# Second layer: the down product in Strassen's seven products too, all up products of 1024 tokens ahead of it

## The chip, the core and the metric

The kernel runs on one core of a Trainium2 chip. The core has a matrix engine (TensorE, PE in the rows, PEld for its weight loads), three element-wise engines (VectorE = DVE, ScalarE = ACT, GpSimd = POOL), a queue engine (SyncE = SP) and 16 DMA engines. The metric is the device time in microseconds, the median of several runs. A profile is one further execution, taken by the hardware profiler; its instructions carry the lines of the kernel, as L642.

## The reference, cut to what matters

```
attn  = memory attention of q, k, v, phi            # 8 x 8 heads, 576 positions, 64 wide
x     = attn as (4608 tokens, 512)
x1    = (silu(x @ w_gate) * (x @ w_val)) @ w_out    # layer 1: 512 -> 1536 -> 512
h     = x1 @ w_in                                   # layer 2, "up":   512 -> 2048
g     = where(h > 0, h, exp(min(h, 0)) - 1)         # ELU
out   = g @ w_out2                                  # layer 2, "down": 2048 -> 512
```

Inputs come as 64-bit floats. The kernel makes 32-bit values of them on the chip and splits each operand of a product into a high and a low part, so that one product is three matmuls: high by high, high by low, low by high.

## The kernel before, in words

Matmuls take a stationary operand of 128 x 128 and a moving one of up to 512 columns, and add into one of eight accumulation banks of PSUM.

**Layer 1** runs over batches of 576 tokens in halves of 288 columns. A first pass over eight batches holds attention, too. Two more passes (the loop that ends in L603) take four blocks of 128 hidden columns each: `gate1`, `val1`, and, two units later (`LAG`), `down2`, which adds into four banks; L525 copies these, and L526 adds the copy to `p1_d` in memory by an accumulating DMA on GpSimd's queue. Between the units the list `conv` is worked off: weights of layer 1, then those of layer 2. For layer 2 `quad_b1`, `quad_b2` and `quad_t` make the seven combinations of a block of `w_in` (VectorE and ScalarE), and `down_w` splits a block of `w_out2` (ScalarE and, at L122 and L123, GpSimd). `store_w2` stores them to memory from ScalarE's queue.

**Layer 2** runs over groups of tokens: 512 tokens first (two halves of 256), then four times 1024 (two halves of 512). The up product is done by Strassen's scheme in Winograd's form: the tokens in two halves, the inputs in two halves of 256 and the hidden columns in pairs of 128 give 2 x 2 blocks, and seven block products take the place of eight. `load3` forms the seven combinations of activations, `fetch_up` brings the weights' (SP queue), and `quad` (L689 to L722) does one of eight steps of 256 hidden columns. A `product` is 6 matmuls, a step 42. Several products add up in the same bank: a partial sum that is needed alone is first copied out by ScalarE (L695, L702, L706), and VectorE adds the copy to another bank (L698, L711, L715). `elu` takes the minimum with zero on VectorE, Exp and Tanh on ScalarE, and a product and a maximum on VectorE.

The down product is plain: for each chunk of 128 tokens (stationary) 16 blocks of weights (moving, 512 output columns) add up in one bank, 3 matmuls a block. Its chunks for the first half of a group are issued between the products of `quad`; the second half's hidden values wait in SBUF (`g2`) and are done after the last step (L757 to L760). Outputs go from L680 or L682 by SP's queue. PSUM is shared as four banks for up products (`ps_up`) and four for down (`ps_acc3`).

The order on each engine is set when the program is built: instructions that are ready go in the order of the program, with those under `high_priority` first; each engine then executes its list strictly in order.

Of the kernel before, what the change touches and what calls it, by code (L numbers as in the profile page):

```python
# [8 lines left out]
F32 = mybir.dt.float32  # L9
# [20 lines left out]
PARTS = (0, 4), (4, 7)  # L30
NWA = 28
NWB = 8
# [5 lines left out]
def attention_moe_moe(ctx: ExitStack, tc: tile.TileContext, qT, phiT, kv, kv4, w1g, w1o, w2, out):  # L38
# [9 lines left out]
    wr_p = ctx.enter_context(tc.tile_pool(name="wr", bufs=4))  # L48
    wt_p = ctx.enter_context(tc.tile_pool(name="wt", bufs=2))
    wa_p = ctx.enter_context(tc.tile_pool(name="wa", bufs=NWA))  # L50
    vx_p = ctx.enter_context(tc.tile_pool(name="vx", bufs=4))
    vt_p = ctx.enter_context(tc.tile_pool(name="vt", bufs=B))
# [21 lines left out]
    up_d = [[dram.tile([128, 2 * (z - a) * 256], F32, name=f"upd{q}_{a}") for a, z in PARTS] for q in range(NQD)]  # L74
    dn_d = [dram.tile([128, 2, DM], F32, name=f"dnd{u}") for u in range(NU2)]
# [17 lines left out]
    def load_w(store, u, i, src, pool, split=True, own=False, raw=None, parts=None):  # L93
# [3 lines left out]
        if parts:  # L97
            pass
        elif split:
            hi = pool.tile([128, 512], F32R, tag="w", name="whi")  # L100
            lo = pool.tile([128, 512], F32R, tag="w", name="wlo")
        else:
            full = pool.tile([128, 512], F32, tag="w", name="wg")
# [3 lines left out]
        with tc.issue_after(last["h"].ins) if "h" in last else nullcontext():  # L107
# [7 lines left out]
            if parts:  # L115
                for part, cs in parts:
                    tt(out=part, in0=v[:, cs], in1=cf[:, cs], op=ALU.add)
                return
            if split:
                act(out=hi, in_=v, func=AF.Copy)  # L120
                part = tt if own else nc.gpsimd.tensor_tensor
                part(out=v, in0=v, in1=hi.bitcast(F32), op=ALU.subtract)  # L122
                part(out=lo, in0=v, in1=cf, op=ALU.add)  # L123
            else:
                tt(out=full, in0=v, in1=cf, op=ALU.add)
        store[u][i] = (hi, lo) if split else full
# [3 lines left out]
    WO = [[None] for _ in range(NU1)]  # L130

    def load_wg(p, k, pool):
        load_w(WG, p, k, w1g[p, k], pool, False, raw=raw.pop((p, k), None))

    def load_wo(u, pool):
        load_w(WO, u, 0, w1o[u], pool, own=u < UA)

    QU = {}
# [7 lines left out]
    def quad_b1(q, pool):  # L146
        t = QU[q] = uq_p.tile([128, 7, 256], F32, tag="uq", name="uq")
        load_w(None, 0, 0, w2[2 * q, :, :1024], None, parts=[(t[:, :2].rearrange("p r c -> p (r c)"), slice(0, 512))])

    def quad_b2(q, pool):  # L150
        t = QU[q]
        b12 = QU[q, 1] = uq_p.tile([128, 256], F32, tag="b12", name="b12")
        load_w(None, 0, 0, w2[2 * q + 1, :, :1024], None, parts=[(b12, slice(0, 256)), (t[:, 4], slice(256, 512))])

    def quad_t(q, pool):
        t, b12 = QU.pop(q), QU.pop((q, 1))
        with tc.issue_after(last["h"].ins):
            tt(out=t[:, 2], in0=b12, in1=t[:, 0], op=ALU.subtract)
            tt(out=t[:, 3], in0=t[:, 4], in1=t[:, 2], op=ALU.subtract)
            tt(out=t[:, 5], in0=t[:, 4], in1=b12, op=ALU.subtract)  # L160
            tt(out=t[:, 6], in0=t[:, 1], in1=t[:, 3], op=ALU.subtract)
            for i, (a, z) in enumerate(PARTS):
                w = pool.tile([128, 2, z - a, 256], F32R, tag=f"u{i}", name="uw")
                act(out=w[:, 0], in_=t[:, a:z], func=AF.Copy)
                tt(out=w[:, 1], in0=t[:, a:z], in1=w[:, 0].bitcast(F32), op=ALU.subtract)
                stores.append((up_d[q][i], w.rearrange("p i r c -> p (i r c)").bitcast(F32)))

    def down_w(u, pool):
        w = [[None]]
        load_w(w, 0, 0, w2[u, :, 1024:], pool)  # L170
        for i in range(2):
            stores.append((dn_d[u][:, i], w[0][0][i].bitcast(F32)))
# [255 lines left out]
    def down1(b, hf, hs, m):  # L428
        ps = ps_gv.tile([128, HS], F32, tag="g", name="pd")
        for u in range(UA):  # L430
            down(ps, WO[u][0], hs[u], slice(128 * m, 128 * m + 128), u == 0, u == UA - 1)
# [13 lines left out]
    for b in range(B):  # L445
# [10 lines left out]
        if b == B - 2:  # L456
            wb_p = ctx.enter_context(tc.tile_pool(name="wb", bufs=NWB))
# [53 lines left out]
    up_p = ctx.enter_context(tc.tile_pool(name="up", bufs=2))  # L511
    st_uq = ExitStack()
    uq_p = st_uq.enter_context(tc.tile_pool(name="uq", bufs=1))

    def down2(q):
# [4 lines left out]
        for m in range(KD):  # L520
            down(accs[m], WO[u][0], hs, slice(128 * m, 128 * m + 128), first, last_u)
# [15 lines left out]
    def load3(t0, n, ops, kks):  # L537
        for kk in kks:
            A = []
            for i in range(2):  # L540
                r = wr_p.tile([128, 2, n], F32, tag="wr", name="x1l")
                for b, o, c0, c in tokens(t0 + i * n, n):
                    nc.sync.dma_start(out=r[:, :, c0:c0 + c], in_=p1_d[b][:, kk::2, o:o + c])
                A += [r[:, 0], r[:, 1]]
            a11, a12, a21, a22 = A
            s1, s2, s3, s4 = (wt_p.tile([128, n], F32, tag=t, name="xs") for t in ("wv", "wc", "wv", "wc"))
            tt(out=s1, in0=a21, in1=a22, op=ALU.add)
            tt(out=s2, in0=s1, in1=a11, op=ALU.subtract)

            def split(r, x):  # L550
                pool = xo_p if r == 6 and n == 512 else wa_p
                hi = pool.tile([128, n], F32R, tag="w", name="xhi")
                act(out=hi, in_=x, func=AF.Copy)
                lo = pool.tile([128, n], F32R, tag="w", name="xlo")
                tt(out=lo, in0=x, in1=hi.bitcast(F32), op=ALU.subtract)
                ops[r][kk] = hi, lo

            split(0, a11)
            split(1, a12)
            split(2, s1)  # L560
            split(3, s2)
            tt(out=s4, in0=a12, in1=s2, op=ALU.subtract)
            tt(out=s3, in0=a11, in1=a21, op=ALU.subtract)
            split(4, s4)
            split(5, s3)
            split(6, a22)

    def new_ops():
        return [[None] * 2 for _ in range(7)]

# [9 lines left out]
    xops = new_ops()  # L580
    for ps in range(2):
        for b in range(B):
            nb, np_ = (b + 1, ps) if b + 1 < B else (0, ps + 1)
            for hf in range(2):
# [3 lines left out]
                for u in range(UA * (ps + 1), UA * (ps + 2)):  # L588
# [8 lines left out]
                    if np_ == 2 and hf == 0 and u % 2 == 1:  # L597
                        load3(0, 256, xops, (u // 2 % 2,))
                    slot += 1
                    while conv and NCONV - len(conv) < slot * NCONV // 126:  # L600
                        conv.pop(0)()
                        if len(stores) > 2:
# [6 lines left out]
    st_p2.close()  # L609
# [187 lines left out]
```

## Time and profile before

| | us |
|---|---|
| median of 3 runs | 1536.23 |
| lowest, highest | 1535.06, 1536.71 |
| profiled execution, its time | 1537.9 |
| profiled execution, first to last instruction (span) | 1536.1 |

Mean granted clock of TensorE over the span: 0.984 of 2.4 GHz; by stretches of 40 us it was 0.74 and 0.83 in the first two, 0.91 from 640 to 680 us, 0.96 from 720 to 800, and 1.00 in all others up to 1520. Its two levels are 1.2 and 2.4 GHz.

How to read it: a row of a group of instructions names the line, the engine, the operation, what it writes and reads (out<-in), the shapes and the count; behind it stand the busy time of the group in us, the mean duration of one in ns, the idle time of the engine just before them, and what ended that. Matmuls overlap, so that their durations add up to more than the time that they take; the time of one is the distance of their starts. 1 KB is 1024 bytes.

### The profile page before, as it was taken

How to read it: one execution, taken by the hardware profiler on the slowest of the kernel's cores; microseconds unless marked ns; L12 is line 12 of the kernel's file. 1: busy time of each engine (PE TensorE's matmuls, PEld its weight loads, DVE VectorE, ACT ScalarE, POOL GpSimd, SP SyncE). 2: the span in 40 equal slices, each digit the busy share in tenths (PEclk: the TensorE clock that was granted, in tenths of full speed). 3: DMA queues.
4: the chain of work that ended last, by engine and by line, in shares of the span. 5: the costliest groups of instructions: out<-in, count | busy, mean ns of one | idle time of the engine just before them, and what ended most of it. 6: DMA issues, size and time to landing. Idle time of an engine off the chain costs nothing.

```text
span 1536.1 us, 25746 instructions
## 1 busy us (share of the span) xinstructions
PE 1478.1 (96%) x9768; PEld 1279.5 (83%) x9768; DVE 1041.3 (68%) x2000; ACT 760.6 (50%) x1579; POOL 109.2 (7%) x87
## 2 busy tenths in 40 slices
PE   4799999999999999989999999999999999999998
PEld 2578888899999999989888888888887888888887
DVE  7988678756666666655776876854677367826662
ACT  4555445544555555444555655633455345624451
POOL 0000000021220000134320000000000000000000
PEclk7899999999999999999999999999999999999999
DMA  9788322436568777878588866576567655566445
GB/s 374 257 293 282 129 94 101 164 126 160 137 162 216 193 188 229 248 209 228 131 251 316 305 213 217 202 266 209 180 209 247 226 180 208 192 231 222 165 135 180
DMA packets 124059, 317.83 MB, mean 207 GB/s; under 512 B 12832, under 2 KB 44576, under 8 KB 114720
## 3 DMA queue, kind: packets, MB, share of 16 engines
q1 hardware_dynamic: 90912, 264.80, 49.9%
q0 software_dynamic: 16896, 18.88, 8.7%
q10 hardware_dynamic: 16128, 32.51, 5.6%
q8 instruction: 77, 1.26, 0.3%
q14 instruction: 46, 0.38, 0.1%
HBM read 245.89 MB, written 70.25 MB: 206 GB/s over the span
## 4 chain that ended last, share of the span: by engine, by line
PE 79%; DVE 6%; DMA 3%; ACT 1%; issue 1%; POOL 0%; ACTq 0%; DVEq 0%; SPq 0%; POOLq 0%
PE acc L675 8%; PE acc L674 8%; PE acc L676 8%; PE pu L642 7%; PE pu L644 7%; PE pu L643 7%; PE acc L203 4%; PE acc L204 4%; PE acc L205 4%; PE pg L198 3%; PE pv L198 3%; PE pg L200 2%; PE pv L200 2%; PE pv L199 2%; PE pg L199 2%; PE pvw L186 2%
## 5 line engine op out<-in xcount | busy, mean ns | idle before, releaser
L675 PE MATMUL acc<-dnw,hh 128*128 128x512 f32 x576 | 224.4, 390 | 0.0
L674 PE MATMUL acc<-dnw,hh 128*128 128x512 f32 x576 | 218.5, 390 | 0.3 <-ACT o L682 0.3
L676 PE MATMUL acc<-dnw,hl 128*128 128x512 f32 x576 | 212.4, 389 | 0.0
L642 PE MATMUL pu<-xhi,upw 128*128 128x512 f32 (+1 forms) x560 | 206.2, 370 | 5.6 <-DVE cc L711 2.6
L643 PE MATMUL pu<-xlo,upw 128*128 128x512 f32 (+1 forms) x560 | 206.4, 369 | 0.0
L644 PE MATMUL pu<-xhi,upw 128*128 128x512 f32 (+1 forms) x560 | 205.5, 369 | 0.0
L209 ACT ACTIVATE hh<-g 128x512 fp32r<-128x512 f32 (+1 forms) x160 | 92.5, 587 | 162.5 <-PE acc L675 106.8
L211 DVE TENSOR_TENSOR hl<-g,hh 128x512 fp32r<-128x512 f32 (+1 forms) x160 | 100.9, 635 | 104.6 <-ACT hh L209 94.6
L203 PE MATMUL acc<-hh,whi 128*128 128x288 f32 x512 | 153.0, 300 | 4.0 <-ACT p1a L525 4.0
L651 ACT ACTIVATE e<-g 128x512 f32<-128x512 f32 (+1 forms) x160 | 90.8, 584 | 132.4 <-DVE g L650 131.3
L230 DVE SCALAR_TENSOR_TENSOR h<-s,pv 128x288 f32<-128x288 f32 x192 | 86.4, 450 | 102.5 <-PE pv L200 77.6
L204 PE MATMUL acc<-hh,wlo 128*128 128x288 f32 x512 | 151.3, 296 | 0.0
L205 PE MATMUL acc<-hl,whi 128*128 128x288 f32 x512 | 150.6, 296 | 0.0
L653 DVE SCALAR_TENSOR_TENSOR g<-e,g 128x512 f32<-128x512 f32 (+1 forms) x160 | 100.6, 640 | 59.1 <-ACT g L652 58.5
L209 ACT ACTIVATE hh<-h 128x288 fp32r<-128x288 f32 x192 | 84.9, 442 | 112.0 <-DVE h L230 108.7
L211 DVE TENSOR_TENSOR hl<-h,hh 128x288 fp32r<-128x288 f32 x192 | 94.2, 491 | 53.8 <-ACT hh L209 53.5
L198 PE MATMUL pg<-at,vw 128*128 128x288 f32 x384 | 119.2, 310 | 11.0 <-ACT at L354 5.7
L642 PEld LDWEIGHTS pu<-xhi,upw 128*128 128x128 f32 x560 | 106.1, 190 | 26.0 <-DVE cc L711 2.8
L674 PEld LDWEIGHTS acc<-dnw,hh 128*128 128x128 f32 x576 | 108.0, 188 | 22.6 <-ACT o L682 0.7
L675 PEld LDWEIGHTS acc<-dnw,hh 128*128 128x128 f32 x576 | 108.2, 188 | 22.2 <-DMA dnw<-dnd 0.4
L676 PEld LDWEIGHTS acc<-dnw,hl 128*128 128x128 f32 x576 | 108.0, 188 | 21.9
L643 PEld LDWEIGHTS pu<-xlo,upw 128*128 128x128 f32 x560 | 106.2, 190 | 18.2
(112 smaller groups left out, 3347.5 us busy)
## 6 DMA issues: line engine op xcount, KB each, us to landing
dnw<-dnd SPq DMA_DIRECT2D x288, 256.0 KB, 3.6
upw<-upd SPq DMA_DIRECT2D x40, 1024.0 KB, 6.9
upw<-upd SPq DMA_DIRECT2D x40, 768.0 KB, 5.1
at<-atd SPq DMA_DIRECT2D x16, 1152.0 KB, 7.2
p1d<-p1a POOLq DMA_DIRECT2D x32, 576.0 KB, 7.1
kvr<-kv SPq DMA_DIRECT2D x32, 512.0 KB, 6.5
wr<-w SPq DMA_DIRECT2D x32, 512.0 KB, 4.8
wr<-w1g SPq DMA_DIRECT2D x24, 512.0 KB, 4.7
```

The lines of the kernel that those rows point to most:

```text
L198: mm(ps, lhsT=wh, rhs=ah, start=g == 0, stop=False)
L203: mm(ps, lhsT=w[0][:, ms], rhs=hs[0], start=start, stop=False)
L204: mm(ps, lhsT=w[1][:, ms], rhs=hs[0], start=False, stop=False)
L205: mm(ps, lhsT=w[0][:, ms], rhs=hs[1], start=False, stop=stop)
L209: act(out=hh, in_=h, func=AF.Copy)
L211: tt(out=hl, in0=h, in1=hh.bitcast(F32), op=ALU.subtract)
L642: mm(ps, lhsT=wh, rhs=xh, start=start and kk == 0, stop=False, skip_group_check=not start)
L643: mm(ps, lhsT=wh, rhs=xl, start=False, stop=False, skip_group_check=not start)
L644: mm(ps, lhsT=wl, rhs=xh, start=False, stop=kk == 1, skip_group_check=not start)
L674: mm(acc, lhsT=hh, rhs=wh, start=u == 0, stop=False)
L675: mm(acc, lhsT=hh, rhs=wl, start=False, stop=False)
L676: mm(acc, lhsT=hl, rhs=wh, start=False, stop=u == NU2 - 1)
```

## The change

- **Tokens.** The first group becomes 512 tokens by the plain scheme, up and down, with activations as moving operand of 512 columns. The four groups of 1024 tokens stay.
- **Order.** In each group all eight up steps come first; the ELU's outputs of all four blocks stay in SBUF (`G`, four tiles). Then seven steps down, one for each of Strassen's products over hidden columns in two halves of 1024: per product 8 blocks of 128 hidden columns x 2 halves of the outputs x 3 matmuls. Here weights are stationary, activations move, and the output is transposed; the host transposes it back. What were chunks of the down product between the up products is gone from there.
- **Within an up step** the products go P1, P5, P6, P2, P3, and P7 and P4 follow between those of the next step. P1, P6, P7 and P4 add up in one bank.
- **Element-wise passes are twice as wide** (1024 columns). The minimum becomes a Relu with scale -1 on ScalarE. The split of hidden values (`split2`) moves into the down steps, and so do the combinations of hidden values (`AFTER`).
- **Weights.** Blocks of `w_out2` get seven combinations like those of `w_in`: `set_load` and `set_split` for both, on VectorE and ScalarE; GpSimd's subtraction and sum are left for blocks of layer 1 alone. 60 tasks instead of 52 are spread over 118 units instead of 126. Fetches are of 1 MB or 768 KB into four buffers.
- **Memory.** SBUF's pools of layer 1 are closed ahead of layer 2 and new ones opened over them; PSUM is shared as six and two banks. A new pool waits until all of the pools that it overlaps are done with. Outputs go by GpSimd's queue.

The diff, cut to its core:

```diff
-        [lambda f=f, q=q: f(q, up_p) for q in range(NQD) for f in (quad_b1, quad_b2, quad_t)] + \
-        [lambda u=u: down_w(u, wb_p) for u in range(NU2)]
+        [lambda f=f, a=a: f(*a) for kind in ("up", "down") for q in range(NQD)
+         for f, a in ((set_load, (kind, q, 0)), (set_load, (kind, q, 1)), (set_split, (kind, q)))]
...
+    def set_split(kind, q):
+        t = SET.pop((kind, q))
+        with tc.issue_after(last["h"].ins):
+            tt(out=t[:, 0:7:6], in0=t[:, 4:6], in1=t[:, 2:5:2], op=ALU.subtract)
+            tt(out=t[:, 1], in0=t[:, 5], in1=t[:, 0], op=ALU.subtract)
+            tt(out=t[:, 7], in0=t[:, 3], in1=t[:, 1], op=ALU.subtract)
+            for r in (0, 4):
+                w = up_p.tile([128, 4, 2, 256], F32R, tag="u", name="uw")
+                act(out=w[:, :, 0], in_=t[:, r:r + 4], func=AF.Copy)
+                tt(out=w[:, :, 1], in0=t[:, r:r + 4], in1=w[:, :, 0].bitcast(F32), op=ALU.subtract)
...
+    def elu(c, src=None):
...
+            act(out=a, in_=c, func=AF.Relu, scale=-1.0)
...
+        act(out=e, in_=a, func=AF.Exp, scale=-1.0)
+        act(out=a, in_=a, func=AF.Tanh, scale=-0.5)
+        stt(out=a, in0=e, scalar=1.0, in1=a, op0=ALU.add, op1=ALU.mult)
...
+            tt(out=c, in0=a, in1=c, op=ALU.max)
...
+        def head(q):
+            z["w0"] = fetch(up_d[q][:, :4])
+            z["p1"], z["p5"] = bank(q % 2), bank(3 + 2 * (q % 2))
+            product(q, "P1", z["p1"], True)
+                z["s1"] = keep(z["p1"])
+            product(q, "P5", z["p5"], True)
+                z["s5"] = keep(z["p5"])
+        def middle(q):
+            product(q, "P6", z["p1"], False)
+                z["s2"] = keep(z["p1"])
+            p2 = bank(2 + 2 * (q % 2))
+            product(q, "P2", p2, True)
+                tt(out=g[:, 0], in0=z["s1"], in1=p2, op=ALU.add)
+            z["w1"] = fetch(up_d[q][:, 5:])
+            product(q, "P3", z["p5"], False)
+                tt(out=g[:, 1], in0=z["s2"], in1=z["p5"], op=ALU.add)
+            elu(g[:, :2])
+        def tail7(q):
+            product(q, "P7", z["p1"], False)
+                tt(out=g[:, 3], in0=z["s5"], in1=z["p1"], op=ALU.add)
+        def tail4(q):
+            product(q, "P4", z["p1"], False)
+                act(out=g[:, 2], in_=z["p1"], func=AF.Copy)
+            elu(g[:, 2:])
...
+        for q in range(NQD):
+            if q:
+                tail7(q - 1)
+            head(q)
+            if q:
+                tail4(q - 1)
+            middle(q)
+        tail7(NQD - 1)
...
+        for n, (name, r, slot) in enumerate(STEPS):
...
+            for p in range(NQD // 2):
+                if p % 2 == 0:
+                    w = fetch(dn_d[p // 2][:, r])
+                hi, lo = split2(g[:, slot], op_p, ("hi", "lo"))
+                if name in AFTER:
+                    o, a, b, op = AFTER[name]
+                    tt(out=g[:, o], in0=g[:, a], in1=g[:, b], op=op)
+                for i in range(2):
+                    for mt in range(2):
+                        three(acc[chain][mt], pair(w, 2 * (p % 2) + i, halves(mt)), (hi[:, i], lo[:, i]),
+                              first, p == NQD // 2 - 1 and i == 1, not start)
```

## Rows read from the trace of the kernel before

**Rows 1.** The page: busy us of each engine, share of the span, instructions.
```profile
PE 1478.1 (96%) x9768; PEld 1279.5 (83%) x9768; DVE 1041.3 (68%) x2000; ACT 760.6 (50%) x1579; POOL 109.2 (7%) x87
```

**Rows 2.** Timeline, matmul pace and VectorE pairs: start us, us, engine, line, operation.
```profile
924.65 0.39 PE L675 MATMUL acc<-dnw,hh 128*128 128x512 f32 x1
...
925.07 1.28 DVE L653 SCALAR_TENSOR_TENSOR g<-e,g 128x512 f32<-128x512 f32 x2
...
929.64 0.39 PE L644 MATMUL pu<-xhi,upw 128*128 128x512 f32 x1
...
785.32 0.28 PE L643 MATMUL pu<-xlo,upw 128*128 128x256 f32 x1
...
788.30 0.28 PE L644 MATMUL pu<-xhi,upw 128*128 128x256 f32 x1
```

**Rows 3.** Groups of matmuls by line and shape, one line of three each.
```profile
L674 PE MATMUL acc<-dnw,hh 128*128 128x512 f32 x576 | 218.5, 390 | 0.3 <-ACT o L682 0.3
...
L642 PE MATMUL pu<-xhi,upw 128*128 128x512 f32 x448 | 174.0, 390 | 2.3 <-DVE g L654 1.5 <-ACT sn L695 0.7
...
L642 PE MATMUL pu<-xhi,upw 128*128 128x256 f32 x112 | 32.2, 290 | 3.3 <-DVE cc L711 2.6 <-DVE cc L715 0.7
```

**Rows 4.** Line 642: durations in ns, first and last start in us.
```profile
L642 PE MATMUL pu<-xhi,upw x560: 274/389/500, 782.9 to 1483.4; 128*128 128x512 f32 x149, 128*128 128x256 f32 x38
```

**Rows 5.** Timeline of the end.
```profile
1530.89 0.39 PE L676 MATMUL acc<-dnw,hl 128*128 128x512 f32 x1
...
1532.06 0.69 DVE L680 COPY o<-acc 128x512 f32<-128x512 f32 x1 [1.41 <-DMA out<-o]
```

**Rows 6.** Waits of TensorE, 783 to 1532 us: total us, times, longest.
```profile
PE pu L642 <- DVE cc L711: 2.6, 1, 2.6
...
PE pu L642 <- DVE cc L715: 0.7, 1, 0.7
```

**Rows 7.** Stretches: us, busy us (instructions) of PE, PEld, DVE, ACT, POOL; clock, DMA.
```profile
640.00:783.00 143.00, 137.03 (x1056) 128.16 (x1055) 87.66 (x173) 71.09 (x172) 52.77 (x39) 0.96 0.76 202
783.00:801.00 18.00, 14.73 (x107) 14.33 (x106) 15.23 (x28) 10.55 (x25) 6.51 (x5) 0.91 0.94 276
...
880.00:960.00 80.00, 80.00 (x354) 66.27 (x353) 57.49 (x102) 42.77 (x77) 0.00 (x0) 1.00 0.64 217
960.00:1000.00 40.00, 39.31 (x173) 32.22 (x172) 35.28 (x62) 28.10 (x50) 0.00 (x0) 1.00 0.58 205
...
1120.00:1160.00 40.00, 38.91 (x171) 31.58 (x170) 34.59 (x60) 25.54 (x46) 0.00 (x0) 1.00 0.63 215
```

**Rows 8.** The page: DMA issues, KB each, median us from issue to landing.
```profile
upw<-upd SPq DMA_DIRECT2D x40, 1024.0 KB, 6.9
```

**Rows 9.** Groups of ScalarE and VectorE, 802 to 1532 us, 512 columns.
```profile
L651 ACT ACTIVATE e<-g 128x512 f32<-128x512 f32 x128 | 77.9, 627 | 124.8 <-DVE g L650 123.9 <-DVE g L653 0.8
...
L695 ACT ACTIVATE sn<-pu 128x512 f32<-128x512 f32 x32 | 19.0, 594 | 21.2 <-PE pu L644 21.1
...
L650 DVE TENSOR_SCALAR g<-cc 128x512 f32<-128x512 f32 x96 | 40.3, 421 | 1.0
...
L698 DVE TENSOR_TENSOR cc<-sn,pu 128x512 f32<-128x512 f32 x32 | 21.9, 683 | 6.9 <-ACT sn L695 4.6 <-PE pu L644 1.3 <-ACT hh L209 0.9
```

**Rows 10.** Groups of 1024 columns, 440 to 620 us.
```profile
L165 DVE TENSOR_TENSOR uw<-uq,uw 128x1024 fp32r<-128x1024 f32 x7 | 8.6, 1226 | 3.3 <-ACT uw L164 3.3
...
L164 ACT ACTIVATE uw<-uq 128x1024 fp32r<-128x1024 f32 x7 | 7.4, 1062 | 3.4 <-DVE uq L159 3.4
```

**Rows 11.** The chain that ended last: start us, us, what.
```profile
641.28 17.85 DMA p1d<-p1a
...
659.68 0.61 PE acc L203
```

**Rows 12.** Users of layer 1's result in memory, 320 to 800 us: ns min/median/max.
```profile
L526 POOL DMA_DIRECT2D p1d<-p1a x32: 1205/1224/1361, 347.8 to 787.0; - x32
```

More of the change, by code (lines that the diff above doesn't have):

```diff
@@ L29 @@
 NQD = NU2 // 2
-PARTS = (0, 4), (4, 7)
-NWA = 28
-NWB = 8
+NWA = 14
+NWB = 4
 NKV = 5
@@ L535, in tokens, with load_x @@
         return out
[L537 to L569, printed above, removed]
+    def load_x(k2):
+        r = wr_p.tile([128, 2, 512], F32, tag="wr", name="x1l")
+        nc.sync.dma_start(out=r, in_=p1_d[0][:, k2:k2 + 2, :512])
+        for k in range(2):
+            w = wa_p.tile([128, 2, 512], F32R, tag="w", name="xs")
+            act(out=w[:, 0], in_=r[:, k], func=AF.Copy)
+            tt(out=w[:, 1], in0=r[:, k], in1=w[:, 0].bitcast(F32), op=ALU.subtract)
+            xsplit[k2 + k] = w
+    xsplit = {}
     LAG = 2
@@ new lines, in split2, with g_tiles, store_out @@
+    def split2(x, pool, tags):
+        hi, lo = (pool.tile([128, 2, T], F32R, tag=t, name=n) for t, n in zip(tags, ("xhi", "xlo")))
+        last["hi"] = act(out=hi, in_=x, func=AF.Copy)
+        last["lo"] = tt(out=lo, in0=x, in1=hi.bitcast(F32), op=ALU.subtract)
+        return hi, lo
+    def g_tiles():
+        return [g_p.tile([128, 4, 2, T], F32, tag="g", name="g3") for _ in range(NQD // 2)]
+    def store_out(t0, d, ps, engine, add=None):
+        o = o3_p.tile([128, T], F32, tag="o", name="o")
+        if add is not None:
+            tt(out=o, in0=add, in1=ps, op=ALU.add)
+        elif engine == "act":
+            act(out=o, in_=ps, func=AF.Copy)
+        else:
+            nc.vector.tensor_copy(out=o, in_=ps)
+        nc.gpsimd.dma_start(out=out[halves(d), t0:t0 + T], in_=o)
@@ new lines, in run_tasks, with spread @@
+    def run_tasks(tasks, upto):
+        while tasks and tasks[0][0] <= upto:
+            with tc.issue_after(last["hi"].ins), tc.issue_after(last["lo"].ins):
+                tasks.pop(0)[1]()
+    def spread(tasks, first, last):
+        tasks = list(tasks)
+        return [(first + (last - first) * i / (len(tasks) - 1), t) for i, t in enumerate(tasks)]
+    xops = {}
+    todo = spread(x_tasks(T, xops), 0, 7)
+    G = g_tiles()
+    for q in range(NQD):
+        w = fetch(up_d[q][:, 2:6])
+        ps = [bank((2 * q + i) % 6) for i in range(2)]
+        for i in range(2):
+            for k in range(KD):
+                x = xsplit[k]
+                three(ps[i], pair(w, 2 * i + k // 2, halves(k % 2)), (x[:, 0], x[:, 1]), k == 0, k == KD - 1)
+        elu(G[q // 2][:, :2, q % 2], ps)
@@ new lines, in attention_moe_moe @@
+    accs = [dbank(0), dbank(1), bank(4), bank(5)]
+    for q in range(NQD):
+        w = fetch(dn_d[q // 4][:, 2:6, q % 4])
+        hi, lo = split2(G[q // 2][:, :2, q % 2], op_p, ("hi", "lo"))
+        for i in range(2):
+            for d in range(KD):
+                three(accs[d], pair(w, 2 * (d // 2) + i, halves(d % 2)), (hi[:, i], lo[:, i]),
+                      q + i == 0, q == NQD - 1 and i == 1)
+        run_tasks(todo, q)
+    for d in range(KD):
+        store_out(0, d, accs[d], ("act", "dve")[d % 2])
```

354 lines of the change are left out of this document (160 added, 194 removed).

## The prediction

> **What bounds the kernel now.** I read the page's busy times first. TensorE is busy for 96% of the span, VectorE for 68% and ScalarE for 50% [rows 1]. Durations of matmuls overlap, so a busy share doesn't say how much TensorE could still give; the starts do. The timeline gives 23 consecutive starts of 512-column matmuls from 924.65 to 929.64 us, 22 steps of 0.2268 us, and 26 starts of 256-column ones from 785.32 to 788.30, 25 steps of 0.1192 us [rows 2]. That stretch of 512-column matmuls runs from down products (activations stationary) into up products (weights stationary) without a change of pace, and both kinds also last the same 390 ns [rows 3]. So it doesn't matter which operand stands still, which the change swaps.
>
> Second, where TensorE doesn't run. The second layer lasts from 782.9 us [rows 4] to the start of the last matmul at 1530.89 plus one step [rows 5], 748.2 us. In it are 1728 + 1344 = 3072 matmuls of 512 columns and 336 of 256 (three lines each, of which [rows 3] shows one): 3072 x 0.2268 + 336 x 0.1192 = 696.7 + 40.1 = 736.8 us. Some 13 matmuls of layer 1 interleaved at its start make 1.7 more. What is left, 9.7 us, is waiting and half clock. About half of it lies in the first 18 us: waits of 2.6 and 0.7 us [rows 6], and a granted clock of 0.91 over 783 to 801 us [rows 7], which costs 18 x 0.09 = 1.6 us; 4.9 in all. The other 4.8 us are short waits where groups meet. So the second layer is bound by the number of matmuls, and a change pays there by executing fewer, as long as ScalarE and VectorE can follow.
>
> **Fewer matmuls.** Down products, four groups of 1024 tokens: 16 x 8 x 3 = 384 matmuls each become 7 products x 8 blocks of K x 2 x 3 = 336, 192 fewer in all: -192 x 0.2268 = -43.5 us. The first 512 tokens lose their seven products: their 336 matmuls of 256 columns (40.1 us) become 8 x 24 = 192 of 512 (43.5 us): +3.5. After the change there are again exactly 3072 of 512 columns and none of 256, so the sum is -40.1 us. (The first group's down products stay 192.)
>
> **First group's stalls.** The waits of 2.6 and 0.7 us were for VectorE's sums out of accumulation banks in 256-token Strassen steps; the new first group has no such sums, reads its banks with two Relu and two max, and rotates over six banks: -4.9 us.
>
> **Layer change.** All of PSUM is now handed over to six plus two banks, and the six reach into those where layer 1 keeps its accumulators. So the first new matmul waits for the last copies out of these (0.4 us each, two beyond the last matmul), where it could start early before: +1.0, between 0 and 3. Weights are no cause: their buffers lie over memory that is free from the end of the weight conversion, some 30 us earlier (10 of the last pass's 128 units), and 1 MB takes 6.9 us [rows 8].
>
> **ScalarE and VectorE in the up steps.** One step of eight is 42 matmuls = 9.53 us of TensorE, without the 24 down matmuls that filled it before. ScalarE has four 512-wide copies out of PSUM at 0.594 [rows 9] and six 1024-wide passes (Relu, Exp, Tanh, twice), for which the 1024-wide copy of layer 1 stands, 1.062 [rows 10]: 2.38 + 6.37 = 8.75 us, 92%. VectorE has three sums at 0.683 [rows 9], four 1024-wide passes at 1.226 [rows 10] and half a further one: 7.57 us, 79%. Both fit, barely. Neighbours that don't depend on each other overlap: two 512-wide VectorE passes took 1.28 us, not 2 x 0.69 [rows 2], so the true load is lower. Who waits: TensorE may not accumulate into a bank before the copy from it is done. From each of the four products of such a bank to the next in the same bank lie 12 matmuls, 2.7 us, in which a copy of 0.6 us must get through ScalarE's queue, behind at most two wide passes. The quads of before left the same 12 to 18 matmuls.
>
> The minimum with zero moves from VectorE (421 ns for 512 columns) to a Relu on ScalarE (near 627) [rows 9]. The Trainium skill, "ScalarE: Activation LUTs", section "Rules for kernel authors", says to do relu, max and min on VectorE and not on ScalarE. The trace agrees on the price. By that rule ScalarE would be the engine that decides; the first rival below works that out from rows.
>
> **In the down steps.** One block is 12 matmuls = 2.72 us. ScalarE splits with 1.06 us; VectorE subtracts with 1.23, and in 12 of 28 blocks forms a combination of activations for another 1.23. The first 16 blocks (43.5 us) also meet the rest of the last up step (5 passes), the first next operand (2) and two output sums: 35 x 1.226 + 1.4 = 44.3 us of durations, less what overlaps. Three operand buffers let TensorE run on for two blocks. The next group's activations are loaded on SP's queue, between weight fetches, and wait there for the buffers of the last ELU; the fetches behind them are due two or more blocks of weights later (four buffers, 5.4 us each): 0.
>
> What does so full an engine cost? The trace has two such stretches: 960 to 1000 us, VectorE 88% busy and ScalarE 70%, TensorE idle for 0.7; and 1120 to 1160, VectorE 86%, TensorE idle for 1.1. At 72%, 880 to 960 us, it idled for nothing [rows 7]. I take 1.0 us for each 40 us of full load. Up steps: 4 x 76.2 = 305 us, 7.6 us. First halves of the down steps: 4 x 43.5 = 174 us, 4.4 us. Together +12 where the old 4.8 go: +7.2 net. The bounds are 0 (as at 72%) and the first rival.
>
> **Layer 1's last pass.** Sums and subtractions of the down weights' conversion move from GpSimd to VectorE: 8 sets x 4096 columns x 1.2 ns (1.226 for 1024) = 39 us over some 430, where VectorE was 61% busy (87.66 of 143 [rows 7]). TensorE there waits for VectorE only when it falls two units (7 us) behind: 0. More bytes are stored, 32 MB for 22, and the stores wait on ScalarE's queue for VectorE's subtraction; behind them stand the next gate's activations, covered by the same two units. What did hurt here: one accumulating store took 17.85 us, beside early weight fetches, and TensorE stood until 659.68 [rows 11]; from 640 to 783 us it was idle for 6.0 us at a mean clock of 0.96, so some 11 us were lost [rows 7]. The early fetches move past the conversion, so this may go, or come back later: 0, from -11 to +13.
>
> **The end.** Outputs go out by GpSimd's queue, whose issue takes 1.22 us each for another store [rows 12], the second behind the first; the old end lost 0.8 us to a busy buffer (1532.06 instead of 1531.3 [rows 5]). +1.5, between -1 and 4.
>
> **Sum** against the profiled span: 1536.1 - 40.1 - 4.9 + 1.0 + 7.2 + 0 + 1.5 = 1500.8 us. That execution took 1537.9 in all, 1.7 above the median of the runs shown, so 35.3 less than 1536.23 is 1500.9: I say 1501.
>
> **Rivals.** *ScalarE sets the pace of the up steps.* For: 92%, and its order is fixed when the program is built, with the copies between wide passes that wait for VectorE. If each step costs its 8.75 us plus one unhidden sum (0.68) and one further wait of that size, 10.1 us, 32 steps add 0.6 each, 18 us for the 7.6 assumed: 1511, and with double waits 1525. Against: at 70 to 88% load hardly anything was lost.
>
> *No new waits.* Overlap keeps both engines at some 85%, TensorE never waits, and layer 1's 11 us go too: 1501 - 12 - 4 = 1485 with a third of these.
>
> *Accumulating stores of layer 1 collide more.* For: 10 MB more of stores. The 11 us lost from 640 to 783 us hold two stalls, some 5.5 us each; two to three more cost 11 to 17: 1512 to 1518. Against: the conversion of up weights, nearly as dense, caused none from 320 to 640 us.
>
> *Slower than before: the splits go serial.* Place: each down block. If copy (1.06), subtraction (1.23) and combination (1.23) run one behind the other instead of ahead of TensorE, a block takes 3.5 us for 2.72, 112 blocks cost 90 us: 1590. It decides once a block loses 0.32 us on average (35.3 / 112). Against: three buffers, and first splits that are ready long before the step begins.
>
> **How the numbers follow.** Forecast (1490 to 1510) 0.60; ScalarE's pace 0.15; no new waits 0.10; colliding stores 0.10; serial splits 0.05. Likeliest: 1501. The range leaves out serial splits, the worst of ScalarE's pace and the best of no new waits: 1485 to 1522. A measurement of this kernel can tell about 0.2% (3 us) from no change; all cases but serial splits are faster by more: faster 0.94, same 0.01, slower 0.05.
>
> **What would show it.** 3072 matmuls of 512 columns in the second layer, 0.227 us apart, in about 711 us; idle time of TensorE before the second, third and fourth product of a bank, ended by ScalarE's copies or VectorE's sum, below 0.3 us a step; ScalarE 85 to 92% busy in up steps, VectorE in the first half of the down steps. Wrong would be: a clock below 1.00 in the second layer, TensorE waiting for a split in every block, or for a weight transfer.

## The result

| | us |
|---|---|
| before, median of the four runs beside it | 1536.30 |
| after, median of 4 runs (lowest, highest) | 1481.05 (1479.32, 1481.42) |
| ratio, 95% interval | 0.9639, 0.9623 to 0.9656 |
| after, span of the profiled execution | 1479.4 |

The change makes the kernel 3.6% faster, 20 us more than forecast and 4 us below the range's low end. The span fell from 1536.1 to 1479.4 us, by 56.7 where the sum had 35.3.

The page of after, busy us of each engine, answers [rows 1]:

```profile
PE 1429.4 (97%) x9432; PEld 1233.7 (83%) x9432; DVE 1095.6 (74%) x1662; ACT 858.9 (58%) x1425; POOL 83.1 (6%) x91
```

9768 - 9432 = 336 matmuls fewer: the 192 fewer down products of the large groups and 336 - 192 = 144 of the first group. Groups of TensorE from 778 to 1476 us by line and shape (busy us, mean ns of one | idle time before them and what ended it) answer [rows 3]:

```profile
L603 PE MATMUL pu<-xhi,w 128*128 128x512 f32 x672 | 261.4, 389 | 0.0
L603 PE MATMUL pd<-xhi,w 128*128 128x512 f32 x288 | 112.0, 389 | 0.0
...
L603 PE MATMUL pu<-xs,w 128*128 128x512 f32 x64 | 25.0, 391 | 2.1 <-ACT p1a L518 2.1
```

With the other two lines of each trio these are 3 x (672 + 288 + 64) = 3072 matmuls, and the one wait stands before the very first. From 778.04 us to the last start at 1474.35 plus one step there pass 696.5 us, 3072 x 0.2267. In the second layer TensorE never waits again.

Stretches of after answer [rows 7] (us, busy us and instructions of PE, PEld, DVE, ACT, POOL; granted clock, DMA): the last pass of layer 1, up steps of the first large group, the first sixteen blocks of its down steps, and the rest of these.

```profile
640.00:775.70 135.70, 134.53 (x1068) 126.05 (x1066) 91.12 (x175) 68.60 (x155) 12.15 (x10) 1.00 0.81 225
...
865.10:941.30 76.20, 76.20 (x338) 63.10 (x337) 57.36 (x61) 62.52 (x79) 1.58 (x3) 1.00 0.64 210
941.30:985.00 43.70, 43.70 (x195) 36.18 (x194) 38.80 (x36) 25.99 (x28) 1.08 (x2) 1.00 0.70 253
```

ScalarE is 62.52 / 76.20 = 82% busy in the up steps and VectorE 38.80 / 43.70 = 89% in the first down blocks, while PE's busy time is the whole stretch and the clock 1.00. In layer 1, 1.2 us of idle time are left of 6.0, and its clock is 1.00 for 0.96.

Term by term, from the two traces:

| term | forecast | measured | difference |
|---|---|---|---|
| fewer matmuls | -40.1 | -40.3 | -0.2 |
| first group's stalls | -4.9 | -4.9 | 0 |
| layer change | +1.0 | +2.2 | +1.2 |
| new waits in full stretches, less the old 4.8 | +7.2 | -4.8 | -12.0 |
| layer 1 | 0 | -8.7 | -8.7 |
| the end | +1.5 | -0.2 | -1.7 |
| sum | -35.3 | -56.7 | -21.4 |

How the measured ones come about: the second layer went from 748.2 us, 1.7 of them matmuls of layer 1, to 696.5, so -50.0, of which 9.7 are the old waits and half clock (4.9 and 4.8). Layer 1 from its first accumulating matmul to its last, those 1.7 us counted in, went from 450.3 to 441.3 us and begins 0.3 later. The gap between the layers is new, and from the last matmul's end to the span's end it is 4.8 us for 5.0. Two terms carry the miss, and the experiments go to them: the new waits, and layer 1.

### The profile page after: what moved, and what is told of

Same layout as the page of the kernel before. It is cut to its first block, busy times and chain, and to the rows that moved or that the text cites. A ratio compares the mean times of both kernels' runs of the same rounds, so it can differ in the third digit from the quotient of the medians.

```text
span 1479.4 us, 23908 instructions
## 1 busy us (share of the span) xinstructions
PE 1429.4 (97%) x9432; PEld 1233.7 (83%) x9432; DVE 1095.6 (74%) x1662; ACT 858.9 (58%) x1425; POOL 83.1 (6%) x91
## 4 chain that ended last, share of the span: by engine, by line
issue 65%; PE 18%; DVE 4%; POOL 3%; ACT 1%; DMA 1%; POOLq 0%; ACTq 0%; DVEq 0%; SPq 0%
PE acc L197 2%; PE acc L199 2%; PE acc L198 2%; POOL p1d L519 1%; PE pg L192 1%; PE pv L192 1%; PE pd L197 1%; PE pv L193 1%; PE pv L194 1%; PE pg L194 1%; POOL out L647 1%; PE pg L193 1%; PE pd L199 1%; PE pd L198 1%; PE pvw L180 1%
## 5 line engine op out<-in xcount | busy, mean ns | idle before, releaser
L605 PE MATMUL pu<-xhi,w 128*128 128x512 f32 x672 | 261.5, 389 | 0.0
L604 PE MATMUL pu<-xlo,w 128*128 128x512 f32 x672 | 261.4, 389 | 0.0
L603 PE MATMUL pu<-xhi,w 128*128 128x512 f32 x672 | 261.4, 389 | 0.0
L632 ACT ACTIVATE xhi<-g 128x1024 fp32r<-128x1024 f32 x120 | 126.7, 1059 | 106.8 <-PE pu L605 63.5
L633 DVE TENSOR_TENSOR xlo<-g,xhi 128x1024 fp32r<-128x1024 f32 x120 | 145.2, 1222 | 45.2 <-ACT xhi L632 45.1
L197 PE MATMUL acc<-hh,wo 128*128 128x288 f32 x512 | 152.3, 299 | 0.5 <-ACT p1a L518 0.5
L198 PE MATMUL acc<-hh,wo 128*128 128x288 f32 x512 | 150.3, 294 | 0.0
L199 PE MATMUL acc<-hl,wo 128*128 128x288 f32 x512 | 148.2, 294 | 0.0
L603 PEld LDWEIGHTS pu<-xhi,w 128*128 128x128 f32 x672 | 126.1, 188 | 26.4
L604 PEld LDWEIGHTS pu<-xlo,w 128*128 128x128 f32 x672 | 126.1, 188 | 26.4
L605 PEld LDWEIGHTS pu<-xhi,w 128*128 128x128 f32 x672 | 126.1, 188 | 25.9
L192 PE MATMUL pg<-at,vw 128*128 128x288 f32 x384 | 118.1, 307 | 10.1 <-ACT at L348 5.7
L192 PE MATMUL pv<-at,vw 128*128 128x288 f32 x384 | 115.8, 301 | 4.2 <-DVE s L217 2.2
L194 PE MATMUL pg<-at,vw 128*128 128x288 f32 x384 | 114.6, 298 | 1.6 <-DVE vw L185 1.6
L193 PE MATMUL pg<-at,vw 128*128 128x288 f32 x384 | 114.4, 298 | 1.1 <-DVE at L349 1.1
L193 PE MATMUL pv<-at,vw 128*128 128x288 f32 x384 | 113.8, 296 | 0.0
L194 PE MATMUL pv<-at,vw 128*128 128x288 f32 x384 | 113.6, 296 | 0.0
```

What stands on the lines that cost most here:

```text
L192: mm(ps, lhsT=wh, rhs=ah, start=g == 0, stop=False)
L193: mm(ps, lhsT=wh, rhs=al, start=False, stop=False)
L194: last["pe"] = mm(ps, lhsT=wl, rhs=ah, start=False, stop=g == 1)
L197: mm(ps, lhsT=w[0][:, ms], rhs=hs[0], start=start, stop=False)
L198: mm(ps, lhsT=w[1][:, ms], rhs=hs[0], start=False, stop=False)
L199: mm(ps, lhsT=w[0][:, ms], rhs=hs[1], start=False, stop=stop)
```

## Experiments

The kernel before was timed again beside these runs: 1534.17 us (median) beside `plain_down`, `act2`, `op1` and `before_late_fetch`, 1534.59 beside `act1`, `min_dve`, `after_p1x2` and `psum_split`, 1534.84 beside the other four. Ratios are against these.

### Is the gain in the second layer the seven products?

`plain_down`: everything as in after (order, wide passes, transposed output), but eight plain block products down (and so without the combinations of hidden values and the kept partial sums).

```diff
-        for n, (name, r, slot) in enumerate(STEPS):
...
+        for n in range(8):
+            a, d, s = n // 4, n // 2 % 2, n % 2
...
-                hi, lo = split2(g[:, slot], op_p, ("hi", "lo"))
-                if name in AFTER:
-                    o, a, b, op = AFTER[name]
-                    tt(out=g[:, o], in0=g[:, a], in1=g[:, b], op=op)
...
+                hi, lo = split2(G[p][:, 2 * a + s], op_p, ("hi", "lo"))
```

> The changed kernel with one part undone: the down product of the four groups by eight plain block products of 48 matmuls, instead of seven. All up steps first, wide passes, the layout of memory and the first group stay. Theory A, the second layer is nothing but its matmuls: 4 x 48 more of 0.2268 us, +43.5 us, 1481.05 + 43.5 = 1524.6, the second layer 740.0 us long without a wait. Then -43.5 of the -55.2 belong to Strassen's products, and -11.7 to everything else together. Theory B, the new order and wide passes gain by themselves or the combinations on VectorE cost: another sum, above 1530 or below 1519.

1523.56 us, ratio 0.9926 (0.9900 to 0.9952), span 1520.6. Its second layer has 3264 matmuls in 740.3 us, 0.2268 each, again without a wait. Against after that is 192 matmuls and 43.8 us: the seven products are worth what their count says. The rest of the change gives the other 11 us, and has paid the 3.5 us by which the plain first group has become longer.

### How much room do ScalarE and VectorE leave?

`act2`: one more 1024-wide pass on ScalarE in each of the two ELUs of a step. `act1`: only in the first of the two.

```diff
         act(out=a, in_=a, func=AF.Tanh, scale=-0.5)
+        for _ in range(more):
+            act(out=a, in_=a, func=AF.Copy)
...
-            elu(g[:, :2])
+            elu(g[:, :2], more=1)
```

> The changed kernel with one more 1024-wide pass on ScalarE in each ELU of an up step (a copy of an intermediate onto itself), two a step. Theory A, durations add up as in the prediction: a step needs 8.75 + 2 x 1.06 = 10.87 us of ScalarE for 9.53 of TensorE, 32 x 1.34 = +43 us, 1524. Theory B, neighbours overlap (busy time in the up steps of the changed kernel is 62.5 us for 8 steps, 7.8 a step, some 0.96 a wide pass): 9.73 us a step, +0.2 x 32 = +6.4 us, 1487, with TensorE's first waits for ScalarE's copies.

> The changed kernel with one more 1024-wide pass of ScalarE in the first ELU of each up step (a copy of an intermediate onto itself). Theory A, load decides: ScalarE's 7.8 us a step become 8.8, still under TensorE's 9.53: no change, 1481; by durations 8.75 + 1.06 = 9.81, +0.28 x 32 = +9, 1490. Theory C, from the run with two more passes: the steps themselves hide any lag, and it is paid once a group, where the down step's fourth block needs the last step's first ELU. There the changed kernel has 0.25 us between the end of the split and TensorE's use of it; a chain longer by 1.1 us leaves a wait of some 0.9 us in each of four groups, +3.4 us, 1484.5, with TensorE waiting in that block and nowhere else in the up and down steps.

`act2` took 1517.78 us (0.9885, 0.9863 to 0.9908), `act1` 1515.68 (0.9886, 0.9868 to 0.9904): the first pass costs some 35 us, the second next to nothing more. If ScalarE's work set the pace of each step, two passes would cost about twice what one does. So it is no pace; `act2` comes near theory A's 1524 us by another mechanism. The up steps of `act2` show it (same columns as above):

```profile
862.00:946.00 84.00, 84.00 (x372) 69.22 (x371) 57.99 (x61) 73.89 (x93) 2.21 (x4) 1.00 0.60 202
```

ScalarE is 88% busy, and TensorE doesn't wait. The waits are elsewhere; TensorE's waits of `act1` from 640 us on (us in total, times, longest; L634 and L635 are L632 and L633 of after), then one group's on the timeline:

```profile
PE pd L603 <- ACT xhi L634: 24.4, 4, 6.1
PE pd L604 <- DVE xlo L635: 1.9, 4, 0.5
PE pu L603 <- ACT p1a L518: 1.3, 1, 1.3
...
```
```profile
953.01 0.80 PE L603 MATMUL pd<-xhi,w 128*128 128x512 f32 x1 [6.09 <-ACT xhi L634]
954.27 0.80 PE L604 MATMUL pd<-xlo,w 128*128 128x512 f32 x1 [0.47 <-DVE xlo L635]
```

In each of the four groups there are two waits, always before the first two matmuls of the fourth down block. This is the block that needs the hidden values of the last up step, the latest that ScalarE and VectorE make. A granted clock of 0.72 follows:

```profile
953.00:964.00 11.00, 10.52 (x34) 8.12 (x35) 10.97 (x11) 5.06 (x6) 0.00 (x0) 0.72 0.85 287
```

The second layer of `act1` is 37.1 us longer than after's: 29.1 in these eight gaps and 8.0 of matmuls at half clock. In after the same place holds by a hair:

```profile
948.05 2.36 DVE L633 TENSOR_TENSOR xlo<-g,xhi 128x1024 fp32r<-128x1024 f32 x2 [2.17 <-ACT xhi L632]
...
949.53 0.39 PE L603 MATMUL pd<-xhi,w 128*128 128x512 f32 x1
```

The first of the two subtractions, 1.22 us long, is the fourth block's. From the end of a block's subtraction to the block's first matmul there are 46.9, 31.9 and 15.6 us for the first three blocks, 0.25 for the fourth, and 0.4 to 2.9 for those behind it.

What expectation C of `act1` missed is the size: 6 us for a pass of 1. ScalarE's list in `act1` tells why:

```profile
942.40 1.06 ACT L617 ACTIVATE et<-g 128x1024 f32<-128x1024 f32 x1 [0.28 <-DVE g L627]
...
951.90 2.95 ACT L634 ACTIVATE xhi<-g 128x1024 fp32r<-128x1024 f32 x3 [2.61 <-DVE g L627]
```

The ELU waits for VectorE's last use of another ELU's temporaries (two exist), the last two ELUs then run interleaved, and the split behind them, in an order fixed when the program is built, waits 2.61 us for the later. `act1_t3` is `act1` with three temporaries (room from the output copies, two for six):

```diff
-    t3_p = ctx.enter_context(tc.tile_pool(name="t3", bufs=2))
+    t3_p = ctx.enter_context(tc.tile_pool(name="t3", bufs=3))
...
-    o3_p = ctx.enter_context(tc.tile_pool(name="o3", bufs=6))
+    o3_p = ctx.enter_context(tc.tile_pool(name="o3", bufs=2))
```

> The run with one more pass of ScalarE in the first ELU of a step (1515.7, a wait of 6.6 us at the fourth block in each group), with three instead of two pairs of temporaries for the ELUs; two instead of six buffers for outputs make room. Theory A, ScalarE's work in the up steps is simply too much by then: the waits stay, 1515. Theory B, the last two ELUs were late because they waited for a pair of temporaries and then ran interleaved: with a third pair the last step's first ELU starts when its input is there, and what is left is the longer chain, some 0.9 us a group: 1485, and if two output buffers hold up VectorE, a few us more.

1488.73 us (0.9695, 0.9673 to 0.9717), with the same number of passes as `act1`:

```profile
948.95 0.50 PE L603 MATMUL pd<-xhi,w 128*128 128x512 f32 x1 [0.28 <-ACT xhi L634]
950.40 0.50 PE L604 MATMUL pd<-xlo,w 128*128 128x512 f32 x1 [0.95 <-DVE xlo L635]
```

1.2 us for 6.6 at the same place, and no half clock after it. The second layer is 9.0 us longer than after's, where `act1`'s is 37.1. By the distances of TensorE's starts, 7.1 of these lie at the four hand-overs and 1.8 at two later blocks. So the pass itself costs some 2 us a group, with whatever the smaller number of output buffers may cost. Two pairs of temporaries made the rest; that the fixed order helped is read from ScalarE's list, and no run changed it.

`min_dve` puts the minimum back on VectorE.

```diff
-            act(out=a, in_=c, func=AF.Relu, scale=-1.0)
+            nc.vector.tensor_scalar_min(out=a, in0=c, scalar1=0.0)
...
```

> The changed kernel with the minimum with zero of the four groups back on VectorE, 1024 columns wide, in place of the Relu on ScalarE (Exp and Tanh with the sign turned). ScalarE loses 2 x 1.06 us a step, VectorE gains 2 x some 0.75. Theory A, ScalarE's load in the up steps decides: faster, up to 1475. Theory B, nothing waits for ScalarE as it is: 1481, no change. Theory C (the fourth block): VectorE, 75% busy in up steps, goes to some 91%; if its lag reaches the fourth block, each us there costs 4, so 1481 to 1490, and the wait ends with VectorE's split.

1500.12 us (0.9774, 0.9759 to 0.9790): 19 us slower than after, where at most 9 were expected. TensorE waits 0.9 and 0.8 us in each group at the fourth block, and 0.2 us in an up step for VectorE's sums, as its waits show:

```profile
PE pd L603 <- ACT xhi L633: 3.6, 4, 0.9
PE pd L604 <- DVE xlo L634: 3.1, 4, 0.8
...
PE pu L603 <- DVE g L765: 1.0, 4, 0.2
```

The second layer is 18.7 us longer than after's: 8.8 at the four hand-overs, some 6 in smaller gaps, and 3.3 of matmuls at half clock behind the last hand-over. The expectation had counted the waits alone. ScalarE was busy for only 48.35 of 76 us in the up steps, VectorE for 60.98 there (57.36 of 76.20 in after) and for 39.19 of 44 in the first down blocks. The Trainium skill, "ScalarE: Activation LUTs", section "Rules for kernel authors", would have relu and min on VectorE. The run says otherwise for this kernel: at the spot that decides, VectorE is the fuller of the two. That its longer list is the reason fits these shares; no run takes it apart.

### How many operand buffers do the down steps need?

`op1` and `op2`: one and two buffers for the splits, for three.

```diff
-    op_p = ctx.enter_context(tc.tile_pool(name="op", bufs=3))
+    op_p = ctx.enter_context(tc.tile_pool(name="op", bufs=1))
```

> The changed kernel with one buffer each for the high and the low part of a down block's activations, instead of three: the serial splits of the prediction's last rival, made by force. A split can start only when TensorE is done with the block before. Theory A, that rival's price: copy 1.06 + subtraction 1.23 stand bare, less some overlap, a block of 2.72 us takes about 5.0: 112 blocks x 2.3 = +258 us, and the first group's eight likewise (+18), 1757; if waits bring the clock to half, more. Theory B, parts of a block (its two halves of 6 matmuls) overlap with the split: well below 1650.

> The changed kernel with two instead of three buffers for the high and the low part of a down block's activations. A split (1.06 + 1.23 us less overlap, some 2.3) then has the time of one block, 2.72 us, instead of two. Theory A, the third buffer is what lets the split run ahead through blocks with combinations: in the 12 blocks with one (another 1.14 us of VectorE) TensorE waits up to 0.8 us each, 4 x 12 x 0.8 = +38 us, and more with half clock. Theory B, one block is enough everywhere: below +5 us.

`op1` took 1922.78 us in its one run. A block now costs some 6.8 us for 2.72, since the copy can't start before the last matmul of the block ahead, and half clock comes on top:

```profile
1001.56 1.06 ACT L632 ACTIVATE xhi<-g 128x1024 fp32r<-128x1024 f32 x1 [5.73 <-PE pu L605]
...
1002.65 1.22 DVE L633 TENSOR_TENSOR xlo<-g,xhi 128x1024 fp32r<-128x1024 f32 x1 [4.30 <-ACT xhi L632]
...
1003.93 0.50 PE L604 MATMUL pu<-xlo,w 128*128 128x512 f32 x1 [0.76 <-DVE xlo L633]
...
1006.15 0.63 PE L604 MATMUL pu<-xlo,w 128*128 128x512 f32 x1
1006.58 0.63 PE L605 MATMUL pu<-xhi,w 128*128 128x512 f32 x1
```

`op2` took 1499.6 us in its one run, 18.5 more than after, and its second layer is 22.1 us longer: 22 waits of 0.2 to 1.2 us, each ended by L633, and some shorter ones, with no half clock. That is between both expectations. So the second buffer keeps the rival of serial splits away, and the third takes the last 20 us or so. The rival's price (3.5 us a block) was too low: the serial block, with its half clock, is twice that.

### Layer 1: is it the early weight fetches?

`before_late_fetch` is before with the second layer's first weight fetches held back until the last conversion load has been issued.

```diff
+            with tc.issue_after(last["wr"].ins):
+                nc.sync.dma_start(out=w.rearrange("p i r c -> p (i r c)").bitcast(F32), in_=up_d[q][i])
```

> The kernel before, with its early weight fetches held back on SP's queue until the last conversion load (767.9 us) has been issued; nothing else. Theory A, those fetches (631.6 to 648.3 us) delayed the accumulating store that took 17.85 us: that store takes 6 to 10 us, the stall of 4.0 us before 659.68 and the 6.8 us at half clock after it go, -6.3 us, ratio 0.996. Theory B, the conversion's own stores and loads did it: the stall stays, ratio 1.000. In both the stall at 731.93 (a split waiting for x) stays.

1535.81 us, ratio 1.0013 (0.9998 to 1.0027): no gain. But the stall went as expected. The store that took 17.85 us [rows 11] takes 9.1, the wait of 4.04 us at 659.68 and the half clock around it are gone, and the pass from its first accumulating matmul to the second layer's first takes 441.9 us for 448.6. The second layer gives it back, with 757.1 us for 748.2:

```profile
787.28 0.38 PE L643 MATMUL pu<-xhi,upw 128*128 128x256 f32 x1 [1.51 <-ACT sn L703]
...
792.95 0.58 PE L643 MATMUL pu<-xhi,upw 128*128 128x256 f32 x1 [2.19 <-DVE cc L712]
...
803.33 0.58 PE L643 MATMUL pu<-xhi,upw 128*128 128x256 f32 x1 [3.28 <-DVE cc L716]
```

These are waits of the 256-token steps, as in [rows 6], but four of them with 7.8 us for two with 3.3, and the clock over 785 to 806 us is 0.75. The traced execution took 1543.56 us, 7.8 more than the median of the twelve; 3.5 of these lie ahead of this pass. So the trace shows where the gain goes, and the medians that it goes, but not how much a usual execution loses in these steps. After has no such steps.

`before_mid_fetch` holds the fetches back less (`loads[-8]`, the eighth load from the end, in place of the last). They are issued from 676.5 to 678.4 us, earlier than the 700 us expected.

> The kernel before, with its early weight fetches held back only until the eighth last conversion load has been issued (about 700 us): past the store that took 17.85 us, well ahead of layer 2. Theory A, the stall of 4.0 us and the half clock at 660 us go as in the run with later fetches, and the first group keeps its old waits, because nothing more than before is in flight there: -6, ratio 0.996. Theory B, another store of layer 1 is hit instead (they come every 13 to 17 us and a fetch pair is 1.75 MB): the stall moves to 700 us, ratio 1.000.

1533.41 us, ratio 0.9986 (0.9973 to 0.9999). The stall moved along with the fetches: the store issued at 681.9 us took 18.8, and TensorE stood at the next one:

```profile
701.28 0.40 PE L204 MATMUL acc<-hh,whi 128*128 128x288 f32 x1 [3.82 <-ACT p1a L526]
```

So the early fetches, 3.5 to 4 MB at once, delay the accumulating store that they meet, in each of the four places where these kernels have them, and with one copy buffer (`p1`) the next copies, and with them the accumulation banks, wait for that store. In `before_late_fetch` they are issued from 765.1 us and meet the store of 772.8, which took 11.9. In after they are issued at 750 us and meet the store of 753.9 us, which took 13.7; TensorE waits 0.45 us there.

### The layer change

`after_p1x2` has two buffers for layer 1's copies; `psum_split` has the six banks for up products as two pools of four and two, so that the first four don't wait for layer 1's accumulators; `both` has both.

```diff
-    p1_p = st_p1.enter_context(tc.tile_pool(name="p1", bufs=1, side="right"))
+    p1_p = st_p1.enter_context(tc.tile_pool(name="p1", bufs=2, side="right"))
...
+    ps_u2 = ctx.enter_context(tc.tile_pool(name="ps_u2", bufs=1, space=PSUM))
...
-        return ps_up.tile([128, T], F32, tag=f"pu{i}", name="pu")
+        return (ps_up if i < 4 else ps_u2).tile([128, T], F32, tag=f"pu{i}", name="pu")
```

> The changed kernel with two buffers instead of one for the copy of layer 1's accumulators that goes to memory by an accumulating store. Theory A, the 2.1 us before the first matmul of layer 2 are the wait of the last copies for the store before them (the copies start at 776.66, when the store of 769.7 has landed): they start at 775.2, and 1.0 to 1.5 of the 2.1 us go; the 0.45 us before 768.11 go, too: -1.5 to -2, ratio to the changed kernel 0.999. Theory B, the copies themselves and the hand-over of banks make the 2.1 us: no change.

> The changed kernel with the six banks of the up products in two pools: four that lie over layer 1's gate, value and weight banks, two over its accumulators. Theory A, the 2.1 us before layer 2 come from handing over six banks at once: the first matmuls need only the first four, so layer 2 starts 2 to 2.3 us earlier, 1479, ratio to the changed kernel 0.9985. Theory B, weights or activations would be late next: less than 1 us.

> The changed kernel with both edits on the layer change: two buffers for layer 1's copies, six up banks in two pools. Theory A, both take the same 2.1 us and the store's last waits (0.45 us): 1477, as with the two pools alone. Theory B, they add up: 1475.

Why the gap is there, from ScalarE's timeline in after:

```profile
776.66 1.32 ACT L518 ACTIVATE p1a<-acc 128x288 f32<-128x288 f32 x4 [4.46 <-DMA p1d<-p1a]
```

The last four copies aren't late because of their own 0.4 us each: they wait until the store ahead of them, issued at 769.7 us, has landed at 776.6 and the only buffer is free. With two buffers the gap is 1.0 us for 2.1; with the banks in two pools, or with both edits, it is gone. From the first accumulating matmul of layer 1 to the last matmul of the kernel it is 1139.8 us in after, 1138.2 in `after_p1x2`, 1136.9 in `psum_split` and 1137.0 in `both`. Times: 1478.39 us (0.9641, 0.9622 to 0.9659), 1477.45 (0.9625, 0.9611 to 0.9639) and 1476.39 (0.9613, 0.9592 to 0.9633). The traces show the gain of 1.6 to 2.9 us and where it is; the ratios' intervals overlap that of after, so the times alone don't. Either edit takes away the same wait, and they don't add up. `both` had the lowest median of all kernels here.

## Why the prediction fell short

**Right.** The count and the pace: 3072 matmuls at 0.227 us, to 0.2 us. That stationary and moving operands may change places at no cost. The first group's stalls, which went with their steps. The direction, and that no transfer of weights would hold TensorE up.

**The step that failed: "1.0 us for each 40 us of full load", +12 us where nothing came.** The step took two stretches of before with full engines and short idle time, and made the one the price of the other. The traces show no such fixed price. In before VectorE works without a pause for 20 us or more in four stretches, each at a change of group, where the next group's operands are formed between the passes of the ELU. In after it does so in seven; the last row is one of these (columns as above):

```profile
859.00:882.80 23.80, 23.24 (x119) 19.57 (x119) 23.41 (x51) 15.16 (x36) 0.00 (x0) 1.00 0.91 310
972.70:1009.70 37.00, 36.31 (x160) 29.76 (x159) 36.89 (x64) 26.18 (x47) 0.00 (x0) 1.00 0.70 239
1136.90:1173.50 36.60, 35.51 (x155) 28.75 (x154) 36.43 (x63) 26.54 (x47) 0.00 (x0) 1.00 0.68 232
1301.80:1334.60 32.80, 32.80 (x146) 27.18 (x145) 32.77 (x57) 24.37 (x44) 0.00 (x0) 1.00 0.61 213
...
975.80:1001.00 25.20, 25.20 (x113) 20.85 (x112) 25.20 (x23) 15.36 (x16) 1.07 (x2) 1.00 0.59 215
```

For VectorE TensorE waited 0.56 us in the first of these, 0.98 in the third and not at all in the second and the fourth; in the seven of after, 158 us in all, it waited for nothing. The 0.7 us of the second stretch, from 993.33, were for one short copy of ScalarE, which began 0.02 us after the product that it reads and had been idle for 0.95 us: load had no part in it. The 0.98 us were for VectorE's L654, as the chain of before has it (start, us, what):

```profile
1147.12 8.41 DMA x1l<-p1d
1155.55 0.69 DVE xs L547
...
1156.77 0.69 DVE g L654
1157.50 0.50 PE pu L642
```

The chain names the transfer of a load behind L547, but VectorE hardly stood for it. In its own list a pass of this size starts some 0.6 us behind the one before it, and L547 starts 0.82 us behind:

```profile
1154.13 0.67 DVE L715 TENSOR_TENSOR cc<-sn,pu 128x512 f32<-128x512 f32 x1
1154.73 0.68 DVE L555 TENSOR_TENSOR xlo<-x1l,xhi 128x512 fp32r<-128x512 f32 x1
1155.55 0.69 DVE L547 TENSOR_TENSOR xs<-x1l 128x512 f32<-128x512 f32 x1
```

So 0.2 of the 0.98 us are the transfer's, and the rest is VectorE's full list. A full list can cost TensorE time, then, but it does so where a result that TensorE needs next stands late in it, and the share of busy time doesn't tell where that is. All this was to be had from the trace before the forecast. `act2` shows the same for ScalarE: 88% cost the up steps nothing. Why the new steps bear full engines is shown in part: with two operand buffers for three the waits come (`op2`). For the banks of the up steps no run shows it.

The load was put too high as well: ten passes by their durations made 8.75 us a step, and the trace of after has 62.52 / 8 = 7.8, 82% where 85 to 92% were to be seen. Independent wide passes of ScalarE there last 1.05 us and start 0.95 apart (VectorE's 1.22 and 1.14). The Trainium skill, "ScalarE: Activation LUTs", section "What ACT_TABLE_LOAD costs", states that consecutive ones overlap by some 93 ns; the trace agrees, with 0.10 us, and the prediction used such an overlap only in words.

The fear behind the step was not idle, though. What full engines put at risk here is one hand-over in each group, with 0.25 us to spare, and one pass more makes it cost some 35 us (`act1`). That place was not named: the text spread the cost over whole stretches.

**Mis-sized: layer 1, 0 where -8.7 came.** The bounds were named (-11 to +13) and the cause of the larger stall was right, as `before_mid_fetch` shows by moving it. Taking 0 weighed "this may go" against "or come back later" evenly. But the prediction had already removed the steps in which it could come back, and after's fetches come when only three accumulating stores are left. `before_late_fetch` took 6.7 us out of this pass alone. The other 2 us or so fit the second stall, 1.85 us at 731.93 in before with 3.4 us at half clock behind it, which after doesn't have; no run takes that one apart.

**The range.** The rival "no new waits" (0.10) is what happened, with four fifths of layer 1's 11 us where it allowed a third, and it was the range's low end. Two errors of one sign, each inside its own bounds, so lie outside a range that took one whole and a third of the other.

**Smaller ones.** The layer change cost 2.2 us, inside its bounds of 0 to 3, by the store that holds the copies rather than by the copies. At the end GpSimd issues in 0.54 us, not the 1.22 that an accumulating store takes [rows 12]; that row was the nearest at hand, but of another kind:

```profile
1474.98 0.54 POOL L647 DMA_DIRECT2D out<-o  x1 [9.46 <-ACT o L644]
1475.76 0.54 POOL L647 DMA_DIRECT2D out<-o  x1 [0.23 <-DVE o L646]
```

**The rivals.** ScalarE's pace is refuted up to 88% load. (Its 1525 for double waits counts 36 us of waits less 12; less the 7.6 of its first number it would be 1529. Nothing hangs on it.) More collisions of stores: there were 10 MB more to store, but of 32 accumulating stores one took over 10 us (13.7), for three in before (17.9 the longest). Serial splits: kept away by the operand buffers, as forecast, of which two would do.

## What to carry to other kernels

A stretch in which an engine is 80 to 90% busy and TensorE idles now and then gives no price for load: look at what ended each idle time, whether the engine named had been idle itself just before, and whether it was as full elsewhere without a wait. A chain names what came last, which can be a small part of the wait; the engine's own list shows how long it really stood. With buffers between, the nearly full engines of this kernel cost nothing on average; what they cost is paid at the hand-over with the least slack (the first block that needs the last values), so work out that slack, and count the temporaries and the fixed order that multiply a small delay. A stall that is removed can be lost again in the next stage's own waits.

## What the runs showed of the hardware

- An accumulating store of 576 KB mostly took 6 to 10 us in layer 1, and 17.9 (before) and 18.8 us (`before_mid_fetch`) beside 3.5 MB of weight fetches. In both cases TensorE stood for about 4 us.
- After waits of 5.6 and 6.1 us the granted clock was at half (1.2 GHz) for 6.8 to 10.2 us, which added 27% (`act1`, 8.0 to 29.1 us) and 38% (`act2`, 10.6 to 28.2) to what the waits took. Short waits differ: after the wait of 2.12 us at 778.04 us in after, the clock stayed at 1.00, and after one of 2.0 us at the same place in `act2` and in `min_dve` it was at half for 3.4 us. In `min_dve` it was so, too, after the last of the four hand-overs, with waits of 0.9 and 0.8 us, and not after the other three.
